# A DeltaNet + maxout FFN kernel: tiled products regrouped, join products with 32 stationary columns, Gram matrices through DRAM in 2 KB rows

## The chip, the cores and the metric

The program runs on one core of a Trainium2 chip. The metric is the device time of one execution in microseconds (us). TensorE (PE) does the matrix products and takes its weights in separate instructions (PEld). VectorE (DVE), ScalarE (ACT) and GpSimd (POOL) do elementwise work. SyncE (SP) and ACT issue the DMAs. All instructions stand in one fixed order per engine: an engine that waits holds up all that stands behind it in its queue.

## The reference

Two stages, all in float32. The first is a delta rule over 768 time steps for 4 x 8 heads of width 48; the second is a feed-forward layer whose hidden value is the largest of three products.

```python
k_n = k / (norm(k) + 1e-06)
for t in range(S):                       # B, H, S, D = 4, 8, 768, 48
    y[:, :, t] = einsum('bhd,bhde->bhe', q[:, :, t], state)
    v_old = einsum('bhde,bhd->bhe', state, k_n[:, :, t])
    state = state + beta[t] * outer(k_n[:, :, t], v[:, :, t] - v_old)
x = y.transpose(0, 2, 1, 3).reshape(B * S, H * D)      # 3072 x 384
h = maximum(maximum(x @ w1, x @ w2), x @ w3)           # 3072 x 768
out = h @ w_out                                        # 3072 x 384
```

## The kernel before

**The work and its pieces.** Time is cut into chunks of C = 64 steps. A *unit* n is half a chunk (two of the four batches, `c, g = divmod(n, 2)`). A *group* m is two chunks, that is four units and 512 rows of x. There are six groups. The recurrence inside a chunk is a triangular system. `solve` (L340) inverts its 32 x 32 diagonal blocks (BL = 32) for a whole group at once, with 62 DVE instructions that each need the one before (L362, L368). The 64 x 64 inverse `ut` is then put together from the two diagonal inverses and a product that joins them: `join_z` (L417) and `join_u` (L431).

**What happens to a unit.** `turn` (L267) transposes k and q with full 128 x 128 products. `gram` (L287) computes k k' and k q' with 64 x 64 tiles of the array, masks the second on DVE into `pt` (L308), copies the first on ACT into `at` (L316), and sends the four 32 x 32-wide diagonal pieces of `at` to DRAM (`at_d`, L327: four DMAs in rows of 128 bytes). With the last unit of a group it reads the blocks back as `x_bl` with one block to a partition (L333). `solve` starts from that: a square root on ACT (L225), a short DVE chain, the 62 steps, then `y_bl` to DRAM (L376), a transposing copy on ACT (L377), its own DMA (L378), and the loads of `ut2`, `t1` and `ut` (L382, L389, L395).

**What happens to a chunk.** `join_z`, `join_u`; `old_k` and `old_q` (L466, L475) multiply with the state; `new` (L481) gives u; `step` (L495) adds to the state; `to_y` (L515); `to_x` (L531) transposes y into `xt`, which the feed-forward of the group reads. All of these but `to_x` use 64 x 64 tiles of the array (32 products of 64 rows, 64 stationary columns and 32 or 48 moving columns). PSUM for them comes from `ps_two`, three buffers.

**The order of work.** `ffn(m)` (L551) is a generator. In each of its 18 steps three full-array products `p_h` give 128 x 512 of one of the three hidden products (ACT copies the first of three, DVE takes the maximum for the other two; two PSUM buffers). Four output steps `p_o` follow. The loop at L691 runs through these 22 steps and puts, after each, pieces of other groups as a table written by hand says: `LINKS` (L671) for the chunks of group m+1 and for `turn` and `gram` of group m+2, fixed step numbers for loads and `prep` (norms of k, L237) of group m+2, and `SOLVE` = 13 for the step at which `solve(m+2)` begins, four of its steps at a time. One pass through the 22 steps is called a *period* below. What a queue then holds is decided by a scheduler that reorders instructions around this order, so pieces can stand a little before or after their step.

In period 0 the table is shifted by nine steps, the weights are still being converted from double precision (`weights`, L185: three DVE, two POOL and one ACT instruction for each of 24 pieces), and ahead of it stands a prologue (L607 to L666) that does the first two groups one after the other. In the prologue the Gram matrices of group 0 go to DRAM on ACT's queue (`bounce`, L614).

In period 5 nothing but the feed-forward is left; in period 4 there are no Gram products and no solve.

Of the kernel before, what the change touches and what calls it, by code (L numbers as in the profile page):

```python
# [9 lines left out]
FP32 = mybir.dt.float32  # L10
U32 = mybir.dt.uint32
I32 = mybir.dt.int32
ALU = mybir.AluOpType

C = 64
# [5 lines left out]
def kernel(  # L21
# [55 lines left out]
    def ps_two(name):  # L77
        return psum.tile([128, 2, 512], FP32, name=name, tag="two", bufs=3)
# [15 lines left out]
    def rows(bb):  # L94
        return slice(C * bb, C * (bb + 1))
# [52 lines left out]

    ut = [const.tile([128, 2, H, C], FP32, name=f"ut{i}") for i in range(NU)]
    ut2 = [const.tile([128, 2, H, BL], FP32, name=f"ut2{i}") for i in range(NU)]  # L150
    t1 = [const.tile([128, 2, H, C], FP32, name=f"t1{i}") for i in range(NU)]

    st = const.tile([128, 2, 2, NP, D], FP32, name="st")
    for t in ut2 + t1 + ut + [st]:
        nc.gpsimd.memset(t, 0.0)


# [129 lines left out]
    def gram(n, parts=(0, 1), queue=nc.sync):  # L287
        kqt, g = kqts[n], n % 2
        p_g = ps_two("p_g")

        whole = len(parts) == 2 and not g
        for j in range(NP):
            for par in range(2):
                for bb in range(2):
                    kq = kqt[rows(par), j, bb ^ g]
                    for i in (0,) if whole else parts:
                        c0 = j * 128 + i * C
                        nc.tensor.matmul(  # L298
                            p_g[
                                rows(bb ^ (g * i)), par, c0 : c0 + C * (1 + whole)  # L300
                            ],
                            kq[:, 0],
                            kq if whole else kq[:, i],
                        )
        p_v = p_g.rearrange("p two (j i t) -> p two j i t", j=NP, i=2)
        if 1 in parts:
            pt = pts[n] = square("pt")
            nc.vector.tensor_tensor(  # L308
                out=by_par(pt), in0=p_v[:, :, :, 1],
                in1=mask[:, None, None, :].to_broadcast([128, 2, NP, C]),  # L310
                op=ALU.mult,
            )
        if 0 not in parts:
            return
        at = ats[n] = square("at")
        nc.scalar.copy(by_par(at), p_v[:, :, :, 0])  # L316


        m = n // 4
        cc = n % 4 // 2  # L320
        if m not in at_d:
            at_d[m] = dram.tile([2, 2, B, H, BL, BL], FP32, name="at_d")
        for half in range(2):
            cols = slice(BL * half, BL * (half + 1))
            for bb in range(2):
                r0 = C * bb + BL * half
                queue.dma_start(  # L327
                    out=at_d[m][half, cc, 2 * bb + g].rearrange("h j i -> j h i"),
                    in_=at[r0 : r0 + BL, :, cols],
                )  # L330
        if n % 4 == 3:
            xs[m] = work.tile([128, BL, BL], FP32, name="x_bl", bufs=1)
            queue.dma_start(  # L333
                out=xs[m], in_=at_d[m].rearrange("f c b h j i -> (f c b h) j i")
            )


    ys = {}
# [1 line left out]
    def solve(m):  # L340


        x = xs[m]
        x_f = x.rearrange("p j i -> p (j i)")
        y = work.tile([128, BL, BL], FP32, name="y_bl")
        y_f = y.rearrange("p c i -> p (c i)")
        nc.gpsimd.memset(y, 0.0)
        bl = small("bl", BL)
        norm(bl, x_f[:, 0 : BL * BL : BL + 1], small("root_bl", BL), small("nt_bl", BL))
        nc.vector.reciprocal(bl, bl)  # L350
        nc.vector.tensor_tensor(out=bl, in0=bl, in1=bl, op=ALU.mult)
        nc.vector.tensor_tensor(out=bl, in0=bl, in1=beta_bl[:, m], op=ALU.mult)
        nc.scalar.copy(y_f[:, 0 : BL * BL : BL + 1], bl)
        nc.vector.tensor_tensor(
            out=x, in0=x, in1=bl[:, None, :].to_broadcast([128, BL, BL]), op=ALU.mult
        )
        yield
        for j in range(BL - 1):
            a, b = j + 1, BL - 1 - j
            tmp = work.tile([128, 256], FP32, name="tmp")  # L360
            t_v = tmp[:, 0 : a * b].rearrange("p (c i) -> p c i", i=b)
            nc.vector.tensor_tensor(  # L362
                out=t_v,
                in0=x[:, j, None, j + 1 :].to_broadcast([128, a, b]),
                in1=y[:, 0:a, j, None].to_broadcast([128, a, b]),
                op=ALU.mult,
            )
            nc.vector.tensor_tensor(  # L368
                out=y[:, 0:a, j + 1 :], in0=y[:, 0:a, j + 1 :], in1=t_v,
                op=ALU.subtract,  # L370
            )
            yield
        queue = nc.sync if m else nc.scalar
        y_d = dram.tile([2, 2, B, H, BL, BL], FP32, name="y_d")
        x_d = dram.tile([2, B, H, BL, BL], FP32, name="x_d")
        nc.sync.dma_start(out=y_d.rearrange("f c b h i j -> (f c b h) i j"), in_=y)  # L376
        nc.scalar.copy(x[0:64].rearrange("p i c -> p c i"), y[0:64])  # L377
        nc.sync.dma_start(out=x_d.rearrange("c b h i j -> (c b h) i j"), in_=x[0:64])  # L378
        for cc in range(2):
            for bb in range(2):  # L380
                b, r0, r1 = 2 * bb, C * bb, C * bb + BL
                queue.dma_start(  # L382
                    out=ut2[cc][r1 : r1 + BL].rearrange("p g h i -> p (g h) i"),
                    in_=y_d[1, cc, b : b + 2].rearrange("b h c i -> c (b h) i"),
                )
            for bb in range(2):
                for g in range(2):
                    rz = C * (bb ^ g)
                    nc.sync.dma_start(  # L389
                        out=t1[cc][rz : rz + BL, g, :, 0:BL],  # L390
                        in_=x_d[cc, 2 * bb + g].rearrange("h c i -> c h i"),
                    )
            for bb in range(2):
                b, r0 = 2 * bb, C * bb
                queue.dma_start(  # L395
                    out=ut[cc][r0 : r0 + BL].rearrange("p g h i -> p (g h) i")[
                        :, :, 0:BL
                    ],
                    in_=y_d[0, cc, b : b + 2].rearrange("b h c i -> c (b h) i"),
                )  # L400
        yield
# [10 lines left out]
        return t[:, :, 0 : H * w].rearrange("p g (h x) -> p g h x", x=w)  # L412


    zs = {}

    def join_z(c):  # L417
        at = [ats.pop(2 * c + g) for g in range(2)]
        p_z = ps_two("p_z")
        p_v = by_head(p_z, BL)  # L420
        for h in range(H):
            for bb, g in TILES:
                nc.tensor.matmul(  # L423
                    p_v[rows(bb ^ g), g, h],
                    at[g][rows(bb), h],
                    ut2[c % NU][rows(bb), g, h],
                )
        z = zs[c] = both("z", BL)
        nc.scalar.copy(z, p_v)

    def join_u(c):  # L431
        z = zs.pop(c)
        p_j = ps_two("p_j")
        p_v = by_head(p_j, BL)
        for h in range(H):
            for bb, g in TILES:
                nc.tensor.matmul(  # L437
                    p_v[rows(bb), g, h],
                    t1[c % NU][rows(bb ^ g), g, h],
                    z[rows(bb ^ g), g, h],  # L440
                )
        nc.vector.tensor_tensor(
            out=ut[c % NU][:, :, :, BL:C], in0=ut2[c % NU], in1=p_v, op=ALU.subtract
        )


    xts, rhss, qss, us, yts = {}, {}, {}, {}, {}
# [196 lines left out]
    for n in (6, 7):  # L644
# [24 lines left out]


    LINKS = {  # L671
# [3 lines left out]
    }  # L675
    FIRST = {0: "u1", 1: "s1", 2: "y1", 3: "x1"}
    BY_CHUNK = dict(
        z=join_z, j=join_u, k=old_k, q=old_q, u=new, s=step, y=to_y, x=to_x
    )
    BY_UNIT = dict(t=turn, g=gram)  # L680
    SOLVE = 13

    def links(m, names):
        for name in names.split():
# [6 lines left out]
    for m in range(GROUPS):  # L691
        shift = 0 if m else 9
        for i, _ in enumerate(ffn(m)):
            if m == 0:
# [4 lines left out]
                if i < shift:  # L699
                    some(solving, 4)  # L700
            i -= shift
            if m + 2 < GROUPS:
                n0 = 4 * (m + 2)
                if 0 <= i < 4:
                    load_k(n0 + i)
                    if i < 3:
                        load_q(n0 + i)
                if i == 5:
                    load_q(n0 + 3)
                if i in (6, 10):  # L710
                    load_v(n0 // 2 + (i - 6) // 4)
                if i in (9, 12):
                    prep(n0 // 2 + (i - 9) // 3)
                if i == SOLVE:
                    solving = solve(m + 2)
                    some(solving, 1)
                if i >= SOLVE:
                    some(solving, 4)
# [32 lines left out]
```

## Time and profile before

| What | Value |
|---|---|
| Time, median of 3 runs | 645.73 us (644.63 to 647.04) |
| The profiled execution's own time | 646.79 us |
| Its span | 645.0 us |
| PE, PEld busy | 559.4 us (87%), 331.7 us (51%) |
| DVE, ACT, POOL busy | 302.4, 144.8, 68.0 us |
| First `p_h` of periods 1 to 5 | 216.1, 311.7, 405.8, 498.3, 578.8 us |
| DMA | 157099 packets, 45.32 MB; 144352 packets under 512 B |

A row of the profile's groups reads: line, engine, operation, written tile <- read tiles, shape, xcount, then busy time and the mean of one in ns, then idle time before it and what ended that. A tile's products count as two instructions each, so 32 products stand as x64. In a timeline a line is start, duration, engine, line, operation, and in brackets the idle time before it with what ended it. SPq and ACTq are DMAs being issued by those engines.

### The profile page before, as it was taken

To read this page: it belongs to the slowest core of one execution; us is meant where nothing else is said; L and a number is where in the kernel's file an instruction comes from. 1 tells how busy PE (TensorE), PEld (TensorE's weight loads), DVE (VectorE), ACT (ScalarE), POOL (GpSimd) and SP (SyncE) were. 2 spreads that over 40 slices of the span, in tenths; PEclk is the share of its full clock that TensorE was granted. 3 is DMA by queue.
4 is the path that set the end of the run, shared out by engine and by line. 5 is a ranking of instruction groups with operands and counts; after the bars stand their busy time and mean duration, and the time that the engine had idled before them with its cause. 6 is when DMAs were issued, how large, how long until landed. Compare 5 with 4: busy or idle time off the path is not lost.

```text
span 645.0 us, 17503 instructions
## 1 busy us (share of the span) xinstructions
PE 559.4 (87%) x7718; PEld 331.7 (51%) x7718; DVE 302.4 (47%) x729; ACT 144.8 (22%) x243; POOL 68.0 (11%) x93
## 2 busy tenths in 40 slices
PE   4334167988999899999899999799999999999997
PEld 3223156755655456556455556455555555554444
DVE  1399459993459513289223399112396122101110
ACT  3224122232431223221223121222122101110001
POOL 6230124333110100000000010000000000000000
PEclk9558558899999999999899999999999999999999
DMA  8872565655263334222434212530202400010002
GB/s 167 159 139 38 152 138 131 146 154 114 50 120 63 92 64 82 38 55 50 100 63 78 53 26 50 109 61 13 51 2 76 73 1 3 1 38 13 0 0 49
DMA packets 157099, 45.32 MB, mean 70 GB/s; under 512 B 144352, under 2 KB 154336, under 8 KB 157024
## 3 DMA queue, kind: packets, MB, share of 16 engines
q1 hardware_dynamic: 144608, 41.95, 30.9%
q10 hardware_dynamic: 12416, 2.26, 2.1%
q8 instruction: 60, 0.98, 0.7%
q14 instruction: 15, 0.12, 0.1%
HBM read 31.56 MB, written 12.58 MB: 68 GB/s over the span
## 4 chain that ended last, share of the span: by engine, by line
PE 69%; DVE 16%; DMA 6%; issue 3%; ACT 2%; POOL 1%; SPq 1%; ACTq 0%; POOLq 0%; DVEq 0%
PE p_h L562 39%; PE p_o L586 12%; DVE tmp L362 5%; DVE y_bl L368 5%; PE p_g L298 3%; PE p_t L276 3%; PE p_j L437 2%; PE p_s L505 2%; PE p_u L487 2%; PE p_y L522 2%; PE p_z L423 2%; PE p_k L459 2%; PE p_q L459 1%; DMA ut<-y_d 1%; DVE mant L208 1%
## 5 line engine op out<-in xcount | busy, mean ns | idle before, releaser
L562 PE MATMUL p_h<-xt,w_sb 128*128 128x512 f32 (+1 forms) x702 | 303.6, 575 | 11.3 <-ACT xt L545 5.8
L562 PEld LDWEIGHTS p_h<-xt,w_sb 128*128 128x128 f32 x702 | 127.2, 191 | 131.0 <-issue 107.3
L572 DVE TENSOR_TENSOR h<-h,p_h 128x512 f32<-128x512 f32 (+1 forms) x78 | 50.2, 643 | 192.3 <-PE p_h L562 192.1
L586 PE MATMUL p_o<-wo_sb,h 128*128 128x384 f32 x288 | 96.4, 489 | 0.7 <-DVE h L572 0.7
L586 PEld LDWEIGHTS p_o<-wo_sb,h 128*128 128x128 f32 x288 | 53.6, 190 | 36.1 <-issue 1.0
L362 DVE TENSOR_TENSOR tmp<-x_bl,y_bl 128x31 f32<-128x31 f32 (+15 forms) x186 | 69.8, 375 | 4.4
L368 DVE TENSOR_TENSOR y_bl<-y_bl,tmp 128x31 f32<-128x31 f32 (+15 forms) x186 | 69.7, 374 | 4.6
L298 PE MATMUL p_g<-kqt 64*64 64x64 f32 (+1 forms) x1280 | 33.0, 252 | 29.6 <-ACT kqt L282 29.5
L298 PEld LDWEIGHTS p_g<-kqt 64*64 64x64 f32 x1280 | 27.5, 150 | 44.8 <-ACT kqt L282 33.6
L570 ACT COPY h<-p_h 128x512 f32<-128x512 f32 (+1 forms) x39 | 21.5, 551 | 119.1 <-PE p_h L562 119.1
L253 POOL TENSOR_TENSOR v_t<-v_t,nrm 128x768 f32<-128x768 f32 x12 | 17.9, 1495 | 225.3 <-DMA v_t<-in_v_dram 95.6
L423 PE MATMUL p_z<-ut,at 64*64 64x32 f32 x768 | 17.6, 232 | 22.4 <-DMA ut<-y_d 22.4
L423 PEld LDWEIGHTS p_z<-ut,at 64*64 64x64 f32 x768 | 15.6, 148 | 33.2 <-issue 28.1
L282 ACT COPY kqt<-p_t 128x1024 f32<-128x1024 f32 (+1 forms) x28 | 24.8, 888 | 17.9 <-PE p_t L276 17.9
L308 DVE TENSOR_TENSOR pt<-p_g,mask 128x512 f32<-128x512 f32 x24 | 16.4, 685 | 22.4 <-PE p_g L298 22.4
L316 ACT COPY at<-p_g 128x512 f32<-128x512 f32 x24 | 13.9, 585 | 53.2 <-DVE pt L308 23.9
L594 ACT COPY o_sb<-p_o 128x384 f32<-128x384 f32 x24 | 11.5, 481 | 62.5 <-PE p_o L586 62.4
L197 ACT ACTIVATE up<-w_bits 128x384 int32<-128x384 uint32 x24 | 13.3, 553 | 44.1 <-POOL w_sb L216 35.5
L276 PE MATMUL p_t<-ident,kpad 128*128 128x128 f32 x96 | 18.4, 322 | 5.2 <-DMA kpad<-in_k_dram 5.2
L216 POOL TENSOR_TENSOR w_sb<-mant,up 128x384 int32<-128x384 int32 x18 | 17.9, 997 | 43.1 <-DVE mant L212 20.4
L527 DVE TENSOR_TENSOR y<-qs,p_y 128x768 f32<-128x768 f32 x11 | 10.5, 951 | 24.8 <-PE p_y L522 24.8
L244 ACT ACTIVATE ksq<-kpad 128x384 f32<-128x384 f32 x24 | 12.6, 525 | 37.2 <-DMA kpad<-in_k_dram 24.0
(67 smaller groups left out, 422.5 us busy)
## 6 DMA issues: line engine op xcount, KB each, us to landing
w_bits<-in_moe_w_dram SPq DMA_DIRECT2D x18, 384.0 KB, 4.6
v_t<-in_v_dram SPq DMA_DIRECT2D x24, 192.0 KB, 3.7
out_dram<-o_sb SPq DMA_DIRECT2D x48, 96.0 KB, 2.2
qpad<-in_q_dram SPq DMA_DIRECT2D x45, 96.0 KB, 3.1
kpad<-in_k_dram SPq DMA_DIRECT2D x44, 96.0 KB, 3.2
y_d<-y_bl SPq DMA_DIRECT2D x6, 512.0 KB, 2.6
at_d<-at SPq DMA_DIRECT2D x80, 32.0 KB, 1.6
x_bl<-at_d SPq DMA_DIRECT2D x5, 512.0 KB, 4.2
```

What stands on the lines that cost most here:

```text
L216: nc.gpsimd.tensor_tensor(out=dst.bitcast(I32), in0=mant_v.bitcast(I32), in1=up_v, op=ALU.add)
L276: nc.tensor.transpose(p_t[:, i, j * 128 : (j + 1) * 128], src[:, 2 * j : 2 * j + 2], ident,)
L282: nc.scalar.copy(kqt.rearrange("p j b i t -> p i (j b) t")[:, some], p_t.rearrange("p i (x t) -> p i x t", t=C)[:, some],)
L298: nc.tensor.matmul(p_g[rows(bb ^ (g * i)), par, c0 : c0 + C * (1 + whole)], kq[:, 0], kq if whole else kq[:, i],)
L362: nc.vector.tensor_tensor(out=t_v, in0=x[:, j, None, j + 1 :].to_broadcast([128, a, b]), in1=y[:, 0:a, j, None].to_broadcast([128, a, b]), ...
L368: nc.vector.tensor_tensor(out=y[:, 0:a, j + 1 :], in0=y[:, 0:a, j + 1 :], in1=t_v, op=ALU.subtract,)
L423: nc.tensor.matmul(p_v[rows(bb ^ g), g, h], at[g][rows(bb), h], ut2[c % NU][rows(bb), g, h],)
L459: nc.tensor.matmul(p_b[rows(bb), par, c0 : c0 + D], kqt[g][rows(par), j, bb ^ g, i], st[rows(par), bb ^ g, g, j],)
L562: nc.tensor.matmul(p_h, w_sb[i][:, t, f * 128 : (f + 1) * 128], xt[:, t, lo : lo + w], start=(t == 0), stop=(t == KT - 1),)
L570: nc.scalar.copy(h, p_h)
L572: nc.vector.tensor_tensor(out=h, in0=h, in1=p_h, op=ALU.max)
L586: nc.tensor.matmul(p_o, hs[f][:, i * 128 : (i + 1) * 128], wo_sb[:, f], start=(f == 0), stop=(f == FT - 1),)
```

## The change

Four things are done at once.

1. *The table.* `LINKS` is rewritten. Products with tiles of the array that stood alone now stand in pairs and threes. In periods 1 to 3 there are 10 runs of tiled products, where there were 18. `join_z` of both chunks moves from steps 0 and 11 to step 3, `gram` of the last unit from step 10 to step 9, `SOLVE` from 13 to 12. Loads of k and q start four steps before the period's end, a group ahead, and loads of v and `prep` are moved a little.
2. *The join products.* Stationary operands have 32 columns where they had 64, outputs 32 partitions where they had 64. z lies in tiles that are zeroed once; `t1` is halved. z and the result are copied in two halves, one by ACT and one by DVE, where there was one instruction of one of them, and POOL copies the lower half of `ut2` into `ut` (two small instructions per chunk).
3. *The Gram matrices.* The whole of `at` goes to DRAM, one DMA per unit and 2 KB to a row. `at_d` has two times as many elements. The output pattern of this DMA is 2 x 64 rows of 512 elements, the input pattern 128 rows.
4. *Reading them back.* `x_bl` is read with four DMAs of 32 partitions, in rows of 128 bytes (1024 rows each). Two of the four depend on the first two units only, and two on the last two.

```diff
-    t1 = [const.tile([128, 2, H, C], FP32, name=f"t1{i}") for i in range(NU)]
+    t1 = [const.tile([128, 2, H, BL], FP32, name=f"t1{i}") for i in range(NU)]
+    zs = [const.tile([128, 2, H, BL], FP32, name=f"z{i}") for i in range(NU)]
...
-            at_d[m] = dram.tile([2, 2, B, H, BL, BL], FP32, name="at_d")
-        for half in range(2):
-            cols = slice(BL * half, BL * (half + 1))
-            for bb in range(2):
-                r0 = C * bb + BL * half
-                queue.dma_start(
-                    out=at_d[m][half, cc, 2 * bb + g].rearrange("h j i -> j h i"),
-                    in_=at[r0 : r0 + BL, :, cols],
-                )
+            at_d[m] = dram.tile([2, C, B, H, C], FP32, name="at_d")
+        queue.dma_start(
+            out=at_d[m][cc].rearrange("j (bb g) h i -> bb g j (h i)", g=2)[:, g],
+            in_=at,
+        )
         if n % 4 == 3:
             xs[m] = work.tile([128, BL, BL], FP32, name="x_bl", bufs=1)
-            queue.dma_start(
-                out=xs[m], in_=at_d[m].rearrange("f c b h j i -> (f c b h) j i")
-            )
+            for half in range(2):
+                part = slice(BL * half, BL * (half + 1))
+                for cc in range(2):
+                    p0 = 64 * half + 32 * cc
+                    queue.dma_start(
+                        out=xs[m][p0 : p0 + 32],
+                        in_=at_d[m][cc, part, :, :, part].rearrange(
+                            "j b h i -> (b h) j i"
+                        ),
+                    )
...
+    def top(t, bb):
+        return t[C * bb : C * bb + BL]
 
     def join_z(c):
...
                 nc.tensor.matmul(
-                    p_v[rows(bb ^ g), g, h],
-                    at[g][rows(bb), h],
+                    top(p_v, bb ^ g)[:, g, h],
+                    at[g][rows(bb), h, 0:BL],
                     ut2[c % NU][rows(bb), g, h],
                 )
-        z = zs[c] = both("z", BL)
-        nc.scalar.copy(z, p_v)
+        nc.scalar.copy(top(z, 0), top(p_v, 0))
+        nc.vector.tensor_copy(top(z, 1), top(p_v, 1))
+        for bb in range(2):
+            low = slice(C * bb + BL, C * (bb + 1))
+            nc.gpsimd.tensor_copy(
+                ut[c % NU][low, :, :, BL:C], ut2[c % NU][low]
+            )
 
     def join_u(c):
...
-                    p_v[rows(bb), g, h],
+                    top(p_v, bb)[:, g, h],
...
-        nc.vector.tensor_tensor(
-            out=ut[c % NU][:, :, :, BL:C], in0=ut2[c % NU], in1=p_v, op=ALU.subtract
-        )
+        u12 = ut[c % NU][:, :, :, BL:C]
+        nc.scalar.mul(top(u12, 0), top(p_v, 0), -1.0)
+        nc.vector.tensor_scalar_mul(top(u12, 1), top(p_v, 1), -1.0)
...
     LINKS = {
-        0: "z0", 1: "k0", 2: "j0", 3: "q0", 4: "u0 t0", 5: "g0", 6: "s0 t1",
-        7: "g1 t2", 8: "k1 t3", 9: "g2", 10: "g3", 11: "z1", 12: "y0", 13: "j1",
-        14: "q1 x0", 15: "u1", 17: "s1", 18: "y1", 20: "x1",
+        0: "k0 q0", 1: "t0 t1", 2: "g0 g1", 3: "z0 z1 t2", 5: "j0 j1", 6: "t3",
+        7: "u0 g2", 9: "s0 g3", 11: "k1 q1", 13: "u1 y0", 14: "x0", 15: "s1",
+        18: "y1", 20: "x1",
     }
...
-    SOLVE = 13
+    SOLVE = 12
...
+            for group, first in ((m + 3, 18), (2, -4 if m == 0 else 99)):
+                if group < GROUPS and first <= i < first + 4:
+                    n = 4 * group + i - first
+                    load_k(n)
+                    if n % 4 < 3:
+                        load_q(n)
             if m + 2 < GROUPS:
                 n0 = 4 * (m + 2)
-                if 0 <= i < 4:
-                    load_k(n0 + i)
-                    if i < 3:
-                        load_q(n0 + i)
-                if i == 5:
+                if i == 2:
                     load_q(n0 + 3)
-                if i in (6, 10):
-                    load_v(n0 // 2 + (i - 6) // 4)
-                if i in (9, 12):
-                    prep(n0 // 2 + (i - 9) // 3)
+                if i in (6, 9):
+                    load_v(n0 // 2 + (i - 6) // 3)
+                if i in (9, 11):
+                    prep(n0 // 2 + (i - 9) // 2)
```

In the lines of the table a letter is a piece (z, j: the two joins; k, q: products with the state; u: new; s: step; y, x; t: turn; g: gram) and a digit is the chunk or unit in its group.

More of the change, by code (lines that the diff above doesn't have):

```diff
@@ L150 @@
     ut2 = [const.tile([128, 2, H, BL], FP32, name=f"ut2{i}") for i in range(NU)]
-    t1 = [const.tile([128, 2, H, C], FP32, name=f"t1{i}") for i in range(NU)]
+    t1 = [const.tile([128, 2, H, BL], FP32, name=f"t1{i}") for i in range(NU)]
+    zs = [const.tile([128, 2, H, BL], FP32, name=f"z{i}") for i in range(NU)]
     st = const.tile([128, 2, 2, NP, D], FP32, name="st")
-    for t in ut2 + t1 + ut + [st]:
+    for t in ut2 + t1 + ut + zs + [st]:
         nc.gpsimd.memset(t, 0.0)
@@ L389, in solve @@
                     nc.sync.dma_start(
-                        out=t1[cc][rz : rz + BL, g, :, 0:BL],
+                        out=t1[cc][rz : rz + BL, g],
                         in_=x_d[cc, 2 * bb + g].rearrange("h c i -> c h i"),
@@ L412, in by_head @@
         return t[:, :, 0 : H * w].rearrange("p g (h x) -> p g h x", x=w)
-    zs = {}
+    def top(t, bb):
+        return t[C * bb : C * bb + BL]
     def join_z(c):
         at = [ats.pop(2 * c + g) for g in range(2)]
+        z = zs[c % NU]
         p_z = ps_two("p_z")
@@ L423, in join_z @@
                 nc.tensor.matmul(
-                    p_v[rows(bb ^ g), g, h],
-                    at[g][rows(bb), h],
+                    top(p_v, bb ^ g)[:, g, h],
+                    at[g][rows(bb), h, 0:BL],
                     ut2[c % NU][rows(bb), g, h],
                 )
-        z = zs[c] = both("z", BL)
-        nc.scalar.copy(z, p_v)
+        nc.scalar.copy(top(z, 0), top(p_v, 0))
[5 more added lines that the diff above has]
+            )
     def join_u(c):
-        z = zs.pop(c)
+        z = zs[c % NU]
         p_j = ps_two("p_j")
```

## The prediction

> **What bounds the kernel now.** First the page's line of engines:
>
> ```profile
> PE 559.4 (87%) x7718; PEld 331.7 (51%) x7718; DVE 302.4 (47%) x729; ACT 144.8 (22%) x243; POOL 68.0 (11%) x93
> ```
>
> TensorE is the fullest engine, but 13% of the span is not its own. The chain of work that ended last, in period 2, shows what small tiles cost it (start, duration):
>
> ```profile
> 328.22 1.08 PE p_q L459 x64
> 329.30 2.77 PE p_h L562 x6
> 332.07 1.08 PE p_u L487 x64
> 333.15 1.02 PE p_t L276 x8
> 334.18 2.58 PE p_h L562 x6
> ```
>
> The same three p_h products take 2.58 behind transposes and 2.77 behind a tiled product: 0.19 us for going back to the whole array. Third, the timeline of period 2, which begins at 311.74:
>
> ```profile
> 363.51 0.58 ACT L316 COPY at<-p_g 128x512 f32<-128x512 f32 x1 [6.31 <-PE p_z L423]
> ...
> 367.99 0.34 SPq L333 DMA_DIRECT2D x_bl<-at_d  x1
> ...
> 371.24 0.26 ACT L225 ACTIVATE root_bl<-x_bl 128x32 f32<-128x32 f32 x1 [4.38 <-DMA x_bl<-at_d]
> ```
>
> ```profile
> 402.83 1.92 ACT L377 COPY x_bl<-y_bl 64x1024 f32<-64x1024 f32 x1 [3.23 <-DVE y_bl L368]
> 404.56 0.51 ACT L594 COPY o_sb<-p_o 128x384 f32<-128x384 f32 x1
> 404.97 0.78 ACT L545 COPY xt<-p_x 128x768 f32<-128x768 f32 x1
> ...
> 405.81 2.84 PE L562 MATMUL p_h<-xt,w_sb 128*128 128x512 f32 x6 [2.31 <-ACT xt L545]
> ```
>
> So a second chain sets the period's length: the last Gram copy, its way through DRAM, the solve (62 DVE steps, 375.7 to 402.8), the ACT copy L377, and behind that in ACT's queue the copy xt that the next period needs. TensorE stands 2.49, 2.23, 2.31 and 1.28 us there at the ends of periods 0 to 3, and up to 1.7 more while p_z waits for ut. Fourth, the DMA view (count, KB, us to landing):
>
> ```profile
> v_t<-in_v_dram SPq DMA_DIRECT2D x24, 192.0 KB, 3.7
> ...
> y_d<-y_bl SPq DMA_DIRECT2D x6, 512.0 KB, 2.6
> at_d<-at SPq DMA_DIRECT2D x80, 32.0 KB, 1.6
> ...
> t<-x_d SPq DMA_DIRECT2D x48, 32.0 KB, 2.0
> ```
>
> **What the Trainium skill says.** TensorEngine Tiling (Array Packing), Key Properties: changing the tiling mode drains TensorE. The 0.19 agrees. TensorE: Matmul & The Clock Gate, LDWEIGHTS: a weight load takes time by its columns. The trace fits: products with 32 and 48 moving columns take the same 1.06 and 1.08, and at half clock (0.5 in that slice) p_j takes 1.93, so the array sets it and not the issue. DMA: Bandwidth & Descriptors, "Why a DMA increments its semaphore by 16 and not by 1": a DMA is spread over the largest number up to 16 that divides the slowest dimension of both patterns. All DMAs of before divide by 16, so no run here shows it. The new at_d output has 2 as its slowest dimension: two engines, 64 rows of 2 KB each.
>
> **The change, part by part.**
>
> *Fewer runs.* A run that is taken away saves the 0.19, and about 0.11 at its start (p_g alone took 1.03; with p_s right behind it 0.92). Eight of 18 go in a period: 2.4 us. In period 4, 13 become 8: 1.5 us.
>
> *Narrow joins.* Four products a period at 1.06. If weight columns set them, half the columns take off at most 0.45; at least 0; a loss is excluded, since no other tiling stands in those runs. I take 0.4: 1.6 us a period. The split copies (ACT and DVE, each under the 0.59 and 0.69 of the whole ones) lie beside p_h. POOL's copies need only ut2; its order in the changed kernel has them right behind the y_bl memset, and POOL is 11% busy. Without that cover u0 would wait by one such copy, about 0.5.
>
> *The last Gram product comes sooner.* In period 2 g3 ended at 359.6, 47.9 from the start, 46.1 without the 1.7 stall. The changed order has before g3: one p_h step less (-2.6), k1 moved behind it (-1.3), z1 and j1 moved ahead (+1.7), narrower z0, j0 (-0.8), six runs fewer (-1.8): 41.3. The copy at waited for p_z of z1 (363.51; it takes over buffers that z1 frees); z1 is now early. So at is written at 42.9 (mask 0.69, copy 0.58, gaps), against 50.7 before.
>
> *Gram to DRAM.* One DMA for four on SP. Its landing is in no row. From at_d (2 KB per engine, 1.6) and y_d (32 KB per engine, 2.6): 33 ns per KB. On 16 engines 16 KB each gives 2.1; on two engines 128 KB each gives 5.8, and shared with the k loads just ahead of it more. I take 5.8: landed at 49.0, where four issues and 1.6 gave 3.9 after the copy before.
>
> *Back to SBUF.* Two of the four x_bl DMAs are early. The last two are 1024 rows each: t with 256 rows lands in 2.0, v_t with 1024 in 3.7, so 3.7 for the first, and 0.6 issue and 1.5 of rows for the second: 5.8, against 3.3 before. x_bl is there at 55, against 57.8 before (59.5 less the stall). On SP ksum, v and k loads wait behind these; their users are later. On ACT root_bl waits, and y_bl, u1 and qs behind it; h of step 12, at 51.8, stands ahead.
>
> *The solve and the end.* From root_bl to the next p_h took 94.1 - 59.5 = 34.6. The changed DVE order has one y addition more inside the solve (0.95), so 35.6. The period: 55 + 35.6 = 90.6. TensorE's own work is 94.1 - 2.3 - 1.7 - 2.4 - 1.6 = 86.1: hidden in the wait. So the merged runs do not pay by themselves; what pays is that the solve begins sooner. The z stall is gone, since z0 now comes 16 us into the period and ut2 lands about 13 after the solve.
>
> Periods 1 to 3 took 95.6, 94.1 and 92.5: -5.0, -3.5, -1.9. Period 4 (no solve, 80.5): 1.5 + 1.6 + the 0.3 wait and a split p_z run: -3.6. Period 5: 0.
>
> *Prologue and period 0.* Four at_d DMAs follow each other on two engines: 13.4 + 4 x 4.2 = 30, in a time when the DMA row shows 8, 8 and 7 tenths busy; say 40 with the other loads. ACT's queue now has x_bl behind them, and root, ksq, kqt and the conversions' `up` behind that; at_d of unit 3 even stands behind the first x_bl. root_bl at 45 instead of 33: +12. ACT no longer spends 1.93 + 4.00 + 4.61 on issuing 16 DMAs, but then it waits. In the changed DVE order the first solve carries 23 conversion instructions for 9 (+14 x 0.47 = 6.6), which are missing later (-6.6). In period 0 k0, q0, t0, t1, g0, g1 leave the crowded stretch from 151.9 to 172.3: -10. The way through DRAM for group 2 is 2.4 + 2.5 longer: +5. Together +7.
>
> *Sum:* +7 - 10.4 - 3.6 = -7. Against the profiled execution (646.79; span 645.0) 639.8; it stood 1.1 above the median, so on the median 645.7 - 7 = 639.
>
> **The rivals.**
>
> A, the forecast: 639, own range 630 to 649, as joins save 0 to 0.45 and the prologue costs 0 to 15.
>
> B, the at_d DMA runs on all 16 engines. Landing 2.1; x_bl at 51.3, root_bl at 51.8 behind h; period 87.4: -8.2, -6.7, -5.1. Prologue: ACT is free some 8 us sooner, of which x_bl's wait in its queue gives back half: -4. Period 4 -3.6. Sum -27.6: 618. For it: no DMA in this trace ever ran on fewer. Against it: the pattern's 2.
>
> C, slower: the two engines are slower than 5.8 because other loads queue on them, and every later DMA on 16 engines has two of its sixteen parts behind them. Each us of landing costs one in each of periods 1 to 3 and four in the prologue: 7 us. At 6.8 us to landing the gain is gone. At 8.5 it is +18.9 on A: 657.
>
> D, the change doesn't reach the path: root_bl comes as late as before, and the waiting DVE holds up the h maxima behind it, so merged runs turn into TensorE waits at the period's end: 645.
>
> **The numbers.** A 0.45, B 0.22, C 0.28, D 0.05. The likeliest is A: 639. The range must reach into B and C: 615 to 657. About 0.5% (3.2 us) is what a measurement of this kernel can tell from no change. Faster by more than that: all of B, 0.7 of A: 0.54. Within: 0.2 of A, D, a little of C: 0.16. Slower: 0.1 of A and most of C: 0.30.
>
> **What would show it.** In the profile after: at_d us to landing, near 2 (B), 6 (A), over 7 (C). root_bl some 55 us into a period; TensorE's wait on xt 3 to 5 us at the ends of periods 0 to 3, larger than before, in A; 1 to 2 in B. p_z and p_j of x64 near 0.65 each. The first root_bl near 45, against 33. I am wrong if periods 1 to 3 are not near 90.6, or if period 0 does not end within 8 us of 223.

## The result and the profile after

The changed kernel takes 665.8 us (median of 4 runs, 665.04 to 667.86), the kernel before 646.1 us. The ratio is 1.0312, 95% interval 1.0281 to 1.0343: slower by 3.1%, where 639 us (615 to 657) was forecast. The span of the profiled execution grew from 645.0 to 664.1 us. This table, read from the timelines, cuts both at the same events:

| Event or length (us) | before | after | difference | forecast |
|---|---|---|---|---|
| first root_bl on ACT | 33.1 | 47.7 | +14.6 | +12 |
| end of the first solve (ACT begins L377 / L381) | 69.9 | 102.6 | +32.7 | +18.6 |
| first p_z | 77.2 | 109.8 | +32.6 | |
| period 1 begins | 216.1 | 248.6 | +32.5 | +7 |
| periods 1, 2, 3 | 95.6, 94.1, 92.5 | 94.0, 90.0, 88.7 | -9.5 | -10.4 |
| period 4 | 80.5 | 76.7 | -3.8 | -3.6 |

(+18.6 is the forecast's 12 and the 6.6 for conversions.) The whole loss arises before the first p_z. From there on the changed kernel is no slower, and from period 1 on it gains about as much as forecast.

First the page's line of engines, and of its DMA part the two lines of the Gram way (out<-in, queue, count, KB each; no landing time stands behind them here):

```profile
PE 543.7 (82%) x7718; PEld 325.1 (49%) x7718; DVE 310.0 (47%) x741; ACT 152.4 (23%) x255; POOL 83.2 (13%) x119
...
at_d<-at SPq DMA_DIRECT2D x20, 256.0 KB
...
x_bl<-at_d SPq DMA_DIRECT2D x20, 128.0 KB
```

TensorE was busy 559.4 us and now 543.7: the change took 15.7 us of work from it, but it now idles 120.4 us of the span instead of 85.6. Second, the chain of waits in period 2 (start, duration, engine, tile, line):

```profile
354.42 2.02 PE p_g L299 x94
356.44 2.77 PE p_h L574 x6
359.21 1.29 PE p_z L430 x98
...
366.67 1.30 PE p_j L449 x98
...
385.27 8.14 DMA at_d<-at
...
394.40 2.42 DMA ksum<-kflip
```

Two narrow p_z or p_j products stand in one run of 1.3 us, where each took 1.06 alone. And for 8.1 us after the issue at 385.27 the solve waits for one DMA, at_d; 5.8 had been worked out, and the four small ones of before landed in 1.6 each (median). Third, the timeline of the same place and of the period's end on ACT:

```profile
384.38 0.58 ACT L317 COPY at<-p_g 128x512 f32<-128x512 f32 x1 [2.24 <-DVE pt L309]
...
396.82 0.26 ACT L226 ACTIVATE root_bl<-x_bl 128x32 f32<-128x32 f32 x1 [2.47 <-DMA ksum<-kflip]
```

```profile
429.51 1.98 ACT L381 COPY x_bl<-y_bl 64x1024 f32<-64x1024 f32 x1 [5.42 <-DVE y_bl L372]
431.31 0.51 ACT L606 COPY o_sb<-p_o 128x384 f32<-128x384 f32 x1
431.72 0.78 ACT L557 COPY xt<-p_x 128x768 f32<-128x768 f32 x1
```

root_bl comes 54.3 us into the period that began at 342.6 (before: 59.5), and 35.7 us later the next period begins. (The profile puts its wait down to ksum, issued right behind the last x_bl; root_bl reads x_bl alone.) So the steady part takes the time that was forecast, though not quite in the way that was forecast, as is shown further below.

Fourth, the place of the loss: ACT and its DMA queue in the prologue.

```profile
15.19 0.53 ACTq L324 DMA_DIRECT2D at_d<-at  x1
16.38 4.80 ACTq L324 DMA_DIRECT2D at_d<-at  x1
...
30.10 0.37 ACTq L334 DMA_DIRECT2D x_bl<-at_d  x1
30.56 2.20 ACTq L324 DMA_DIRECT2D at_d<-at  x1
32.80 10.32 ACTq L334 DMA_DIRECT2D x_bl<-at_d  x3
43.22 0.22 ACT L226 ACTIVATE root<-ksum 128x16 f32<-128x16 f32 x1 [21.42 <-DMA x_bl<-at_d]
...
47.65 0.24 ACT L226 ACTIVATE root_bl<-x_bl 128x32 f32<-128x32 f32 x1
```

The at_d issued at 15.19 lets the first x_bl go only at 30.1, 15 us later; ACT does nothing for 21.4 us, and TensorE waits 27.4 us for the transposed k that ACT should copy (kqt, next at 43.76). Then the DVE inside the first solve:

```profile
75.47 0.36 DVE L200 TENSOR_SCALAR mant<-w_bits 128x384 uint32<-128x384 uint32 x1 [0.90 <-DMA w_bits<-in_moe_w_dram]
...
81.63 0.36 DVE L200 TENSOR_SCALAR mant<-w_bits 128x384 uint32<-128x384 uint32 x1 [2.29 <-DMA w_bits<-in_moe_w_dram]
81.91 0.41 DVE L366 TENSOR_TENSOR tmp<-x_bl,y_bl 128x252 f32<-128x252 f32 x1
...
95.72 0.36 DVE L200 TENSOR_SCALAR mant<-w_bits 128x384 uint32<-128x384 uint32 x1 [3.09 <-DMA w_bits<-in_moe_w_dram]
```

Conversions stand between the solve's steps and wait for weights, and the solve waits with them. The chain of waits shows how late those weights are:

```profile
85.56 10.06 DMA w_bits<-in_moe_w_dram
```

10.1 us for a load whose median before was 4.6.

### The profile page after: what moved, and what is told of

Same layout as the page of the kernel before. It is cut to its first block, busy times and chain, and to the rows that moved or that the text cites. A ratio compares the mean times of both kernels' runs of the same rounds, so it can differ in the third digit from the quotient of the medians.

```text
span 664.1 us, 17537 instructions
## 1 busy us (share of the span) xinstructions
PE 543.7 (82%) x7718; PEld 325.1 (49%) x7718; DVE 310.0 (47%) x741; ACT 152.4 (23%) x255; POOL 83.2 (13%) x119
## 4 chain that ended last, share of the span: by engine, by line
PE 56%; DVE 19%; DMA 16%; issue 4%; ACT 2%; SPq 1%; ACTq 1%; POOL 1%; DVEq 0%; POOLq 0%
PE p_h L574 31%; PE p_o L598 12%; DMA at_d<-at 6%; DVE y_bl L372 5%; DVE tmp L366 4%; DMA w_bits<-in_moe_w_dram 4%; DMA x_bl<-at_d 2%; PE p_g L299 2%; PE p_t L277 2%; DMA kpad<-in_k_dram 2%; PE p_u L499 2%; PE p_s L517 1%; DMA ut<-y_d 1%; PE p_y L534 1%; DVE mant L213 1%
## 5 line engine op out<-in xcount | busy, mean ns | idle before, releaser
L574 PEld LDWEIGHTS p_h<-xt,w_sb 128*128 128x128 f32 x702 | 131.4, 195 | 136.0 <-issue 117.5
L372 DVE TENSOR_TENSOR y_bl<-y_bl,tmp 128x31 f32<-128x31 f32 (+15 forms) x186 | 72.9, 392 | 4.2
L598 PEld LDWEIGHTS p_o<-wo_sb,h 128*128 128x128 f32 x288 | 53.7, 190 | 40.5 <-DVE h L584 4.8
L366 DVE TENSOR_TENSOR tmp<-x_bl,y_bl 128x31 f32<-128x31 f32 (+15 forms) x186 | 68.1, 366 | 4.4
L299 PE MATMUL p_g<-kqt 64*64 64x64 f32 (+1 forms) x1280 | 33.1, 256 | 44.4 <-ACT kqt L283 44.3
L430 PE MATMUL p_z<-ut,at 64*32 64x32 f32 x768 | 10.2, 203 | 37.0 <-DMA ut<-y_d 37.0
L430 PEld LDWEIGHTS p_z<-ut,at 64*32 64x32 f32 x768 | 8.9, 114 | 42.4 <-POOL y_bl L351 31.4
L439 POOL COPY ut<-ut 32x512 f32<-32x512 f32 x24 | 15.0, 625 | 114.6 <-DMA ut<-y_d 113.9
L606 ACT COPY o_sb<-p_o 128x384 f32<-128x384 f32 x24 | 11.6, 484 | 72.0 <-PE p_o L598 70.0
L483 DVE TENSOR_TENSOR v_t<-v_t,p_k 128x768 f32<-128x768 f32 x11 | 10.5, 952 | 24.5 <-PE p_k L471 16.5
L245 ACT ACTIVATE ksq<-kpad 128x384 f32<-128x384 f32 x24 | 12.5, 522 | 33.6 <-DMA kpad<-in_k_dram 17.0
```

Of the source, the lines that this page charges most:

```text
L299: nc.tensor.matmul(p_g[rows(bb ^ (g * i)), par, c0 : c0 + C * (1 + whole)], kq[:, 0], kq if whole else kq[:, i],)
L366: nc.vector.tensor_tensor(out=t_v, in0=x[:, j, None, j + 1 :].to_broadcast([128, a, b]), in1=y[:, 0:a, j, None].to_broadcast([128, a, b]), ...
L372: nc.vector.tensor_tensor(out=y[:, 0:a, j + 1 :], in0=y[:, 0:a, j + 1 :], in1=t_v, op=ALU.subtract,)
L430: nc.tensor.matmul(top(p_v, bb ^ g)[:, g, h], at[g][rows(bb), h, 0:BL], ut2[c % NU][rows(bb), g, h],)
L574: nc.tensor.matmul(p_h, w_sb[i][:, t, f * 128 : (f + 1) * 128], xt[:, t, lo : lo + w], start=(t == 0), stop=(t == KT - 1),)
L598: nc.tensor.matmul(p_o, hs[f][:, i * 128 : (i + 1) * 128], wo_sb[:, f], start=(f == 0), stop=(f == FT - 1),)
```

## The experiments

Theory 1: the at_d DMA on two engines costs the time, by its own landing and by what it holds up. Theory 2: the DVE's new order, with 23 conversion instructions in the first solve for 9, does it, however at_d is written. A third reading puts it on the table and the narrow joins. All runs in one table (us; "period 1" is its begin, "1-3" the sum of the three periods; the last five columns are read from the profiled execution of each; the ratio stands with its 95% interval, against runs of the kernel before that were made together with that kernel, medians 645.4 to 646.1):

| Kernel | time | ratio to before | first root_bl | first p_z | period 1 | 1-3 | period 4 |
|---|---|---|---|---|---|---|---|
| before | 645.9 |  | 33.1 | 77.2 | 216.1 | 282.2 | 80.5 |
| changed | 665.8 | 1.031 (1.028-1.034) | 47.7 | 109.8 | 248.6 | 272.7 | 76.7 |
| e1_split | 632.3 | 0.978 (0.975-0.982) | 32.1 | 87.5 | 220.7 | 266.8 | 76.7 |
| e2_gram_only | 693.7 | 1.075 (1.070-1.080) | 46.5 | 108.9 | 249.2 | 296.2 | 79.8 |
| e3_old_gram | 629.9 | 0.974 (0.970-0.979) | 33.2 | 77.3 | 212.3 | 268.8 | 76.7 |
| e4_gram_split | 652.9 | 1.010 (1.006-1.013) | 32.9 | 88.2 | 224.9 | 279.4 | 81.1 |
| e5_two_k2 | 667.8 | 1.033 (1.031-1.035) | 48.2 | 110.4 | 248.4 | 275.1 | 76.7 |
| e6_split_hold | 627.3 | 0.971 (0.969-0.973) | 32.7 | 80.0 | 215.5 | 266.5 | 76.7 |
| e7_split_wide | 639.4 | 0.991 (0.987-0.994) | 32.2 | 87.6 | 223.8 | 270.7 | 78.3 |
| e8_split_first | 656.2 | 1.015 (1.011-1.018) | 32.1 | 96.1 | 239.8 | 271.6 | 76.7 |
| e9_hold | 668.0 | 1.034 (1.032-1.036) | 47.0 | 104.0 | 248.9 | 274.7 | 76.7 |
| e10_split_two | 646.6 | 1.000 (0.997-1.003) | 31.3 | 86.7 | 227.4 | 276.2 | 76.7 |
| e12_dummy | 671.6 | 1.040 (1.035-1.044) | 50.4 | 115.0 | 251.4 | 275.8 | 76.7 |

**e1_split: at_d over 16 engines.**

```diff
-        queue.dma_start(
-            out=at_d[m][cc].rearrange("j (bb g) h i -> bb g j (h i)", g=2)[:, g],
-            in_=at,
-        )
+        for bb in range(2):
+            queue.dma_start(
+                out=at_d[m][cc, :, 2 * bb + g].rearrange("j h i -> j (h i)"),
+                in_=at[rows(bb)].rearrange("p h i -> p (h i)"),
+            )
```

> The changed kernel, only at_d written with two DMAs per unit, each 64 rows on both sides, so spread over 16 engines. Theory 1 (the two engines cost the time): at_d lands in 2 to 3 us instead of 14.8 (prologue) and 8 (periods 1 to 3); first root_bl near 35 instead of 47.7, waits for w_bits inside the first solve gone (6 us), 2 us in each of periods 1 to 3: about 640 us. Theory 2 (the new order of the DVE puts conversions into the first solve, however at_d is written): the first solve still takes about 45 us from its first product, about 655 us. The order of this kernel has 25 conversion instructions in the first solve (the changed kernel 23, the kernel before 9).

632.3 us: 33.5 us from one DMA pattern, faster than before, and faster than either theory had put it (640 and 655). Its at_d, in the view of the tile:

```profile
DMA to landing us min/median/max: 2.2/3.2/6.1
```

27.9 of the 33.5 us are gone before period 1. But the first p_z is still 10.3 us later than before, with root_bl no later: a part of theory 2 stands, and e6 prices it.

**e2_gram_only, e3_old_gram, e4_gram_split: which part.** e2 is the kernel before with points 3 and 4 of the change alone (the diff below, and the four x_bl DMAs); e3 is the changed kernel with the same lines turned back; e4 is e2 with the two at_d DMAs of e1.

```diff
-            at_d[m] = dram.tile([2, 2, B, H, BL, BL], FP32, name="at_d")
+            at_d[m] = dram.tile([2, C, B, H, C], FP32, name="at_d")
...
+        queue.dma_start(
+            out=at_d[m][cc].rearrange("j (bb g) h i -> bb g j (h i)", g=2)[:, g],
+            in_=at,
+        )
...
```

> The kernel before with the changed way of the Gram matrices through DRAM alone (one at_d DMA per unit, four x_bl DMAs). If that part makes the whole loss of the first 255 us: first p_z near 110 as in the changed kernel, +35 there, and 4 to 7 us in each of periods 1 to 3, whose end waits for the solve: about 695 to 705 us. If the table or the joins make the loss: first p_z near 80, about 665 us.

> The changed kernel with the Gram matrices sent as before (four at_d DMAs of 128-byte rows per unit, one x_bl DMA): table and narrow joins alone. If the loss is the Gram path's: first p_z near 77, periods 1 to 3 near 86 to 87 (TensorE's own work), about 615 us. If the table and the joins do not pay by themselves: about 640 us.

> The kernel before with the changed Gram path but at_d in two DMAs per unit over 16 engines. Theory 1 (two engines): prologue nearly as before, periods 1 to 3 some 2 us longer by the four x_bl DMAs: about 652 us. Theory 2 (conversions in the first solve, 25 instructions in this kernel's order): +16 us in the first solve, first p_z near 95: about 667 us.

The Gram part alone costs 47.8 us: 33 before period 1, 14 in periods 1 to 3. Without it the rest of the change gains 16 us (e3); the hoped 615 was missed by 15, 11 of which are the three periods, which came to 89.6 on average and not to 86. e4 hit 652. So the table and the joins are not to blame, and the Gram part is bad mostly for its two engines: 40.8 of the 47.8 us go with them (e2 against e4).

**e5_two_k2: the number of engines or the number of DMAs.** Two DMAs as in e1, but with a gap in at_d between blocks of 32 rows, so that the slowest dimension of the output is 2.

```diff
-            at_d[m] = dram.tile([2, C, B, H, C], FP32, name="at_d")
+            at_d[m] = dram.tile([2, 2, BL + 1, B, H, C], FP32, name="at_d")
...
+                out=at_d[m][cc, :, 0:BL, 2 * bb + g].rearrange("f j h i -> f j (h i)"),
```

> Two at_d DMAs per unit as in the split kernel (632 us), but each with an output pattern of 2 x 32 rows (a gap in at_d keeps the two from being one), so that its slowest dimension is 2. If the number of engines costs the time: at_d lands in 6 to 8 us, first root_bl near 45, about 655 to 668 us as the changed kernel. If having two DMAs instead of one made the split kernel faster: about 632 us, at_d at 2 to 4 us.

667.8 us, as the changed kernel. In its chain of waits at_d takes

```profile
16.04 10.07 DMA at_d<-at
...
204.94 9.99 DMA at_d<-at
...
295.90 8.48 DMA at_d<-at
...
388.64 7.95 DMA at_d<-at
...
478.09 7.27 DMA at_d<-at
```

So it is the pattern and not the number of DMAs: e5's at_d DMAs differ from e1's in nothing but the split of 64 rows into 2 x 32 and the gap. This fits the Trainium skill, DMA: Bandwidth & Descriptors, "Why a DMA increments its semaphore by 16 and not by 1": a slowest dimension of 2 leaves two engines, one of 64 gives sixteen. The same section says that these DMAs take the lowest-numbered engines, so that all at_d would share the same two; e5's two DMAs together being no faster than one agrees. The runs show the times; the profile does not name the engines that a DMA used.

**e8_split_first, e10_split_two: which group's at_d.** The two DMAs for group 0 alone, or for groups 0 and 1.

```diff
+        if m == 0:        # e10: if m < 2
+            for bb in range(2):
...
+        else:
             queue.dma_start(
```

> The changed kernel, with at_d split over 16 engines for group 0 alone; groups 1 to 5 keep the one DMA on two engines. If the loss comes with the landings of group 0: first root_bl near 32, first p_z near 92 (w_bits still waits behind the at_d of group 1), period 1 begins near 232, periods 1 to 3 as in the changed kernel: about 648 us. If it comes with those of group 1 and later: above 658 us.

> The changed kernel, with at_d split over 16 engines for groups 0 and 1; groups 2 to 5 keep the two engines. If the w_bits loads of the first solve wait on the two engines behind the at_d of group 1: w_bits lands in 4 us instead of 10, first p_z near 88, period 1 begins near 224, total near 641 us. If group 2's at_d in period 0 matter more: first p_z near 88 but period 1 begins after 230, 648 us.

Period 1 begins at 248.6, 239.8, 227.4 and 220.7 as none, one, two and all groups are split; the whole times fall by 9.6, 9.6 and 14.3 us from step to step. Group 0 alone moves root_bl by 15.6 us, but period 1 only by 8.8: e8's 648 was missed by 8. Its first solve takes 48.5 us from the product of x_bl and bl on (L358 in the changed kernel, where it takes 45.8). Two w_bits loads of 9.8 and 10.0 us are on its chain, and its order has 31 conversion instructions in that solve. Group 1's at_d is read only after the first solve and yet is worth 12.4 us at period 1, 9.4 of them already at the first p_z, in which its own reader has no part. In e10 none of those loads is among the long pieces of the chain, and the same solve takes 39.9 us with 25 conversion instructions; its 646.6 us lie between its two expectations. So before period 1 a slow at_d costs time through what it does to other work, not only through its own reader. How much of that is late loads and how much the other order on the DVE was not separated.

**e12_dummy: two busy engines without a reader.** e1 with a third DMA per unit that writes `at` on two engines to a scratch tensor, which nobody reads.

```diff
+        at_s[n] = dram.tile([C, B, H, C], FP32, name="at_s")
+        queue.dma_start(
+            out=at_s[n].rearrange("j (bb g) h i -> bb g j (h i)", g=2)[:, g],
+            in_=at,
+        )
```

> The split kernel, and behind each unit's two at_d DMAs a third one that writes at once more on two engines, to a scratch tensor that nobody reads. It leaves the Gram way as fast as in the split kernel and makes two engines busy. If the loads that are spread over all 16 engines wait for those two: w_bits lands in 8 us or more, period 1 begins some 12 us later than in the split kernel, about 645 to 650 us. If only at_d's own landing counts: 632 to 635 us.

671.6 us: 39.3 us above e1, and above the changed kernel; less than half of that was expected. And the Gram way did not stay as fast as in e1, though that had been expected: the first root_bl comes at 50.4, not at 32.1. The waits of SP's DMA queue between 10 and 110 us show one way in which a DMA without a reader costs time (engine line <- releaser: us, times, longest):

```profile
SPq L251 <- DMA at_s<-at: 6.0, 1, 6.0
SPq L118 <- DMA at_s<-at: 4.9, 1, 4.9
```

ksum (L251) and v_t (L118) have nothing to do with at_s. In the text of the built program eight semaphores serve the DMAs of SP and ACT in turn, and a DMA waits for the one before it on its semaphore: this v_t is the eighth DMA behind the first at_s, this ksum the eighth behind the second. So a slow DMA stops the queue eight DMAs later, and all that stands behind it there. The other way is in its chain:

```profile
81.32 14.27 DMA w_bits<-in_moe_w_dram
```

This is 14.3 us from the first issue for weights that took a median of 4.0 and at most 6.5 in e1: late after they are issued, too. Which share of this is parts that queue on the two engines, and which is issues held back (the three w_bits issues that begin there took 8.8 us together), was not separated. No run has a third DMA spread over 16 engines, so what a further 256 KB per unit cost by themselves is not shown either.

**e6_split_hold, e9_hold: the conversions in the first solve.** One tiny copy out of the solve's last column, ahead of the seventh conversion, keeps it and those after it behind the solve on the DVE; e6 adds this to e1, e9 to the changed kernel.

```diff
+            if idx == 6:
+                nc.vector.tensor_copy(
+                    mant.bitcast(FP32)[:, 0:1], ys[0][:, 0, BL - 1 : BL]
+                )
```

> The split kernel, with one tiny copy out of the last column of the first solve ahead of the seventh conversion, so that conversions from the seventh on stand behind the first solve on the DVE (9 conversion instructions in the solve instead of 25). If the conversions stretch the solve and the time is not given back: first solve 30 us instead of 40, first p_z near 78, about 622 to 625 us. If the conversions are needed just as much later (weights for the first p_h): first p_z near 78 but first p_h near 112 as in the split kernel, 632 us.

> The changed kernel, only with the conversions from the seventh on held behind the first solve as above (8 conversion instructions in the solve instead of 23). If their place in the DVE's order costs 15 us on its own: first solve 31 us instead of 46, first p_z near 95, about 651 us. If the time is given back by later conversions: first p_h near 134 again, about 665 us.

e6 takes 627.3 us, 5.0 less than e1 (622 to 625 had been hoped for): the first solve takes 30.6 us from the product of x_bl and bl on instead of 40.0, the first p_z comes 7.5 and period 1 5.2 us sooner. Theory 2 is right for 5 us. e9 met neither of its expectations in full: the same hold brings the first p_z forward by 5.8 us, and period 1 not at all (248.9). Its solve still takes 40.1 us with 8 conversion instructions, with DVE waiting 9.6 us on a root that waits for ksum in SP's queue, and the rest is given back. As long as at_d goes over two engines, the hold gains nothing (668.0 us). e6 beats both kernels. Its period 2:

```profile
305.50:394.90 89.40, 86.17 (x1290) 49.33 (x1288) 46.50 (x111) 23.71 (x38) 5.71 (x7) 1.00 0.35 72
```

The first number after the stretch is its length, then TensorE's busy time: 86.2 of 89.4 us, and the forecast had worked out 86.1 for TensorE's own work.

**e7_split_wide: the joins.** e1 with `join_z`, `join_u` and `t1` of the kernel before (64 stationary columns, z and ut written whole).

```diff
-                    top(p_v, bb ^ g)[:, g, h],
-                    at[g][rows(bb), h, 0:BL],
+                    p_v[rows(bb ^ g), g, h],
+                    at[g][rows(bb), h],
```

> The split kernel (632 us) with the joins of the kernel before: 64 stationary columns, z and ut written whole. If the narrow joins save their 0.4 us per product as forecast, 1.6 us in each of periods 1 to 4 and some 2 in the prologue: about 641 us. If they save nothing that the end sees: 632 us. Against the Gram-split kernel with the table of before (653 us) what is left is the table's own part.

639.4 us, where 641 was expected: the narrow joins are worth 7.1 us. In the two profiled executions, which are 8.8 apart, 3.9 are in periods 1 to 3, 1.6 in period 4 and 3.1 before. Between e4 and e7 only the table with its loads and its earlier solve differs: 13.5 us, 8.7 in periods 1 to 3 and 2.8 in period 4.

## Why the prediction was wrong

**Where it was right, and where by luck.** Period 4, -3.6, measured -3.8. Narrow joins, 1.6 us a period, measured 1.3 on average in periods 1 to 3 and 1.6 in period 4. The first root_bl, +12, measured +14.6. For periods 1 to 3, "55 + 35.6 = 90.6" gave 271.8 us together; 272.7 were measured, with root_bl 56.7, 54.3 and 53.7 us into the periods, and 37.3, 35.7 and 35.0 from there to the next one.

That root_bl came so near to 55 is partly luck. In period 2 at_d landed in 8.1 us and not in 5.8 (by the forecast's own sum (8.1 - 1.5) / 128 KB, an estimate of 52 ns per KB, where 33 was taken from the 16-engine rows), but from that landing to root_bl it took 3.4 us and not 6: the two misses cancel.

The path to the period's end was another one, too. TensorE was to wait 3 to 5 us there behind the solve and the ACT copy L381. It waits 1.9 us for o_sb behind that copy at the start of period 1 (the 2.49 of before was such a wait, too), 0.6 for xt at the start of period 3, and not at all at the other two ends. It waits earlier, in p_x for y. These are its waits in periods 1, 2 and 3:

```profile
PE p_x L551 <- DVE y L539: 3.4, 1, 3.4
PE p_h L574 <- ACT o_sb L606: 1.9, 1, 1.9
...
PE p_x L551 <- DVE y L539: 1.9, 1, 1.9
...
PE p_x L551 <- DVE y L539: 2.4, 1, 2.4
PE p_h L574 <- ACT xt L557: 0.6, 1, 0.6
```

y stands on the DVE behind the solve's first steps, and these wait for root_bl (6.1 us in period 2). Behind that p_x TensorE works on to the period's end, where it is ready within 1 us of the solve and the copies behind it. So root_bl reaches the next period on two paths of nearly the same length, of which the forecast had one.

"So the merged runs do not pay by themselves" was not tested: with the Gram way of e1 the table gives some 3 us a period, but it also begins the solve sooner.

**The step that failed** is "Prologue and period 0 ... Together +7": +32.5. Period 0 ended at 248.6, where the forecast was to count as wrong outside 8 us of 223. In its own terms:

| Term | forecast | measured |
|---|---|---|
| root_bl later | +12 | +14.6 |
| the first solve longer, from root_bl to its end | +6.6 | +18.1 |
| to the first p_z | 0 | -0.1 |
| from there to period 1: -6.6 (conversions done), -10 (less crowded), +5 (Gram way of group 2) | -11.6 | -0.1 |
| sum | +7 | +32.5 |

The second term counted 14 conversion instructions at 0.47 us and took their weights as there. In e1, where weights are in time, the solve from root_bl is 12.5 us longer than before, 10.1 of them from the product of x_bl and bl on. There stand 16 more conversion instructions and ten small ones of the norms, and the solve's own steps last longer (on average 0.46 us where they took 0.39). The DVE is busy 39.0 of these 40.0 us and waits for no other engine, so this is work and not waiting. The other 5.6 us came with the two engines; the three waits on w_bits shown above add up to 6.3.

The fourth term promised that period 0 would give back 11.6 us; it gave 0.1. TensorE's work from the first p_z to period 1 fell from 119.9 to 114.7 us, but its idle time there rose from 19.0 to 24.1. In e1 the work fell to 112.6 and the idle time rose to 20.6: 133.2 us for the stretch against 138.9. So 16 engines gave 5.7 of the 11.6, and two engines took 5.6 of these back. Why the idle time did not shrink with the work was not tested.

**The rivals.** C named the sign, and a mechanism that fits the runs, "every later DMA on 16 engines has two of its sixteen parts behind them", but its price, 7 us for each us of at_d's landing, saw only the readers of at_d. By that price 8.1 us to landing is 655 (and 8.5 is 657.9, not 657). e8, e10 and e12 show that the loads of others and the DVE's order are hit as well, in the prologue, where weights are fetched during the first solve. B (618) was tried as e1: 632.3. Of these 14 us, 8.6 arise before period 1, 5 of them by the conversions in the first solve (e6), and 4.6 in periods 1 to 3; there TensorE works 86.2 of 89.4 us in e6, which leaves little for a faster Gram way to gain. D did not happen as a whole, since root_bl came 4 to 6 us sooner in periods 1 to 3; but a DVE that waits for root_bl and holds up what stands behind it is what delays y. The range ended where C ended, and C was not extended by a second victim; that left the time outside.

**The account.** In this order: the Gram way on 16 engines costs the kernel before 7.0 us (e4), the table gives 13.5 (e7), the joins give 7.1 (e1), two engines instead of sixteen cost 33.5. The sum is +19.9, and 665.8 - 645.9 is 19.9; it must come out, as each step is the difference of two neighbours in one row of kernels. The shares depend on the order: with the old table and joins two engines cost 40.8 us (e2 against e4), and with the new ones the Gram way on 16 engines stands at 632.3 against 629.9 for the old way (e1 against e3), where single runs of e3 reach up to 632.5. In neither pair does sending the whole of `at` in 2 KB rows gain anything.

## What to carry to other kernels

Before a DMA pattern is made of fewer and longer rows, look at the slowest dimension of both its sides: here a 2 in front, which two DMAs instead of one would have avoided, cost 33 us in a kernel where the rows of this transfer had become 16 times longer. When a DMA becomes slow, price not only its reader, but all that is loaded in the same stretch and all that stands behind its semaphore in the queues. And a scheduler can move other work when a transfer's issues change (e4, with nothing but the Gram way changed, has 25 conversion instructions in the first solve for 9): compare each engine's order around the longest dependent chain (here the first solve), and hold filler work out of it if need be.

## What the runs showed of the hardware that was not expected

A DMA of 256 KB with a slowest dimension of 2 took 7.8 to 8.1 us from issue to landing in periods 1 to 3 and some 15 in the prologue; of the two DMAs with 64 that carry the same bytes in e1, each took a median of 3.2.

Halving the stationary columns of a 64-row tile took the weight load from 135 to 107 ns (medians) and a product from 219 to 193 ns. These overlap, so the pace says more: the 32 products of a join took 1.06 us and take 0.65, two fifths less for half the columns.

A copy of 32 partitions x 512 took what one instruction of 128 x 512 had taken: 0.57 against 0.59 us on ACT, 0.69 on the DVE against 0.69 for the subtraction before. The forecast had put the halves below the wholes; split by partitions over two engines, they saved neither engine any time.

In the first solve single DVE instructions that otherwise take 0.3 to 0.4 us last 1.1 when POOL's addition of a conversion (1.0 us) runs beside them, in both kernels (at 84.38 in the changed one, at 44.04 before). That they disturb each other is only inferred from the times.
